# Two blocks of V of one group per layer moved to partitions 0 to 63, in eight transfers on ACT's queue

## The chip, the cores and the metric

The kernel runs on one core of one Trainium2 chip. A core has engines that run their own instruction streams and meet at semaphores: TensorE (PE, matrix products into PSUM), VectorE (DVE), ScalarE (ACT), GpSimd (POOL) and SyncE (SP, here the issuer of transfers). Sixteen DMA engines bring data from HBM into SBUF, a memory of 128 partitions. SP and ACT can each issue transfers, each on a queue of its own that all sixteen engines serve. The metric is the device time of one execution in microseconds; less is better.

## What is computed

One token passes twice through an attention layer over a cache of 4096 keys and an MLP. Everything is float32; the caches K and V (32 heads, 4096 keys, 128 numbers each, 67 MB each) are read twice, once in each layer.

```python
def _A_ref(x, k_cache, v_cache, wq, wo):
    ...
    q = (x @ wq).reshape(B, Sq, H, Dh).transpose(0, 2, 1, 3)
    scores = jnp.einsum("bhqd,bhkd->bhqk", q, k_cache) * (Dh ** -0.5)
    p = _softmax(scores, axis=-1)
    o = jnp.einsum("bhqk,bhkd->bhqd", p, v_cache)
    return o.transpose(0, 2, 1, 3).reshape(B, Sq, H * Dh) @ wo
def _B_ref(x, w1, b1, w2, b2):
    h = _gelu(jnp.einsum("bsd,df->bsf", x, w1) + b1)
    return jnp.einsum("bsf,fd->bsd", h, w2) + b2
x = A_x
x = x + _A_ref(_layernorm(x), A_k_cache, A_v_cache, A_wq, A_wo)
x = x + _B_ref(_layernorm(x), B_w1, B_b1, B_w2, B_b2)
x = x + _A_ref(_layernorm(x), A_k_cache, A_v_cache, A_wq, A_wo)
x = x + _B_ref(_layernorm(x), B_w1, B_b1, B_w2, B_b2)
```

## The kernel before

The 32 heads are worked in eight groups of four (g; n is a group's turn). Layer 0 goes through g = 0 to 7, layer 1 through 7 to 0, so that what is in SBUF at the end of layer 0 (V of g = 7 whole, parts of K and V of g = 6) needn't be read again. All tiles lie in one SBUF array, `arena`; a transfer's place in it is given by hand as a column (`k_home`, `v_home`, in units of `NC` = 2048 columns, 8 KB; `BLOCK` = 8 NC is a whole K or V tile of a group, 128 partitions x 64 KB).

One group's turn is: `stream("k", ...)` loads K, and `scores` (L211) multiplies its eight chunks with the query, 32 products of 512 columns into the PSUM tile `pS`; `softmax` (L216) finds the maximum on DVE, makes the exponential on ACT (L223), turns the weights around with four transposes on PE (L225) and copies them to `pt` (L227); `stream("v", ...)` loads V, and `values` (L239) makes 32 products of 4 x 512 into `pO`: of each chunk, four blocks b of 128 keys for each of four heads j. `scaled_out` (L244) and `head_out` (L266) take the group's result through its part of wo into `pB`, and `queries` (L201) makes the next group's query. Between these, `idle` (L367) issues products whose result nobody uses; six of them stand behind the scores of layer 0's first group (L418 to L420).

Every transfer goes through `load` (L83), on SP's queue in the order in which the program is written, 128 partitions at a time. In the middle of a layer the order is K, V, then wo and the next wq together (`in_w`, L473), then the next group's K. A transfer is issued when the place that it writes is free: V of a group when the products on the K that lay there are done, w when the queries that used the old one are done, in layer 0 the next K when the V that lay there has landed and been used.

The framework gives each transfer the next of eight semaphores (DMAHW0 to DMAHW7), in turn over the order in which it schedules the program, whatever engine issues it. A transfer on a semaphore that is in use waits, on its issuing engine, until the transfer before it on that semaphore has landed. With SP alone, eight transfers lie between two uses.

Of the kernel before, what the change touches and what calls it, by code (L numbers as in the profile page):

```python
# [17 lines left out]
P = 128  # L18
# [3 lines left out]
G = 8  # L22
J = 4
C = 8
# [3 lines left out]
U = 512  # L28
KEPT = 6

NC = 4 * U
BLOCK = 8 * NC

STAY = 5 * NC
SPARE = 2 * BLOCK + STAY
HELD = SPARE + 2 * NC
# [14 lines left out]
FILL = 3  # L51
LAST = ((0, 4), (4, 6), (6, 7))
LAST_IDLE = {3: 1, 5: 1, 6: 1}
WHOLE, HALVES = ((0, 8),), ((0, 4), (4, 8))
VAR_AT = 1


@with_exitstack
def decode_layers(ctx: ExitStack, tc: tile.TileContext, k, v, w, w1, w2, out):
    nc = tc.nc  # L60
# [20 lines left out]
    arena = const.tile([P, ARENA], F32, name="arena")  # L81

    def load(at, src):  # L83
        t = arena[:, at : at + src.shape[-1]]
        tc.keep_in_program_order(nc.sync.dma_start(t, src))
        return t
# [41 lines left out]
    row, _ = wq_at(0)  # L128
# [3 lines left out]
    ident = ctile("ident", P)  # L132
# [7 lines left out]
    pS, pO, pB = (psum.tile([P, 512], F32, name=n) for n in ("pS", "pO", "pB"))  # L140
# [75 lines left out]
    def softmax(sc, nsc, p):  # L216
        nc.vector.tensor_reduce(mx[:, 0:1], pS, axis=AX.X, op=ALU.max)  # L217
        mt, m, bias = small("mt", 32), small("m"), small("lr", 32)
        nc.vector.transpose(mt, mx)
        nc.vector.tensor_reduce(m, mt[:, :C], axis=AX.X, op=ALU.max)  # L220
        nc.vector.tensor_scalar(mb[:, :C], m.to_broadcast([P, C]), nsc, None, op0=ALU.mult)
        nc.vector.transpose(bias, mb)  # L222
        nc.scalar.activation(p, pS, AF.Exp, bias=bias[:, 0:1], scale=sc, accum_out=mx[:, 0:1])  # L223
        for b in range(4):
            nc.tensor.transpose(pT[:, b].rearrange("p j r -> p (j r)"), p[:, P * b : P * (b + 1)], ident)  # L225
        pt = work.tile([P, J, C, 4], F32, name="pt")
        nc.vector.tensor_copy(pt, pT[:, :, :, :C].rearrange("p b j c -> p j c b"))  # L227
        lt, l, lr, rl = small("mt", 32), small("l"), small("lr", 32), small("rl")
        nc.vector.transpose(lt, mx)  # L229
        nc.vector.tensor_reduce(l, lt[:, :C], axis=AX.X, op=ALU.add)  # L230
        nc.vector.tensor_copy(lt, l.to_broadcast([P, 32]))
        nc.vector.transpose(lr, lt)
        nc.vector.reciprocal(rl, lr[:, 0:1])
        return pt, rl

    def by_head(vt):
        return vt.rearrange("p b (j d) -> p j b d", j=J)

    def values(i, pt, vt, c, of=C):  # L239
        for j in range(J):  # L240
            nc.tensor.matmul(pO[32 * j : 32 * j + 4, :], pt[:, j, c, :], by_head(vt)[:, j],  # L241
                             start=(i == 0), stop=(i == of - 1))
# [127 lines left out]
    for layer in range(2):  # L370
# [17 lines left out]
        r = rstd_of(ss, pN[:, 1:2])  # L388
# [4 lines left out]
        for n, g in enumerate(order):  # L393
# [6 lines left out]
            if layer == 1 and n == 0:  # L400
                tiles = [(c, here["k", g, c]) for c in range(C)]
            elif layer == 1 and n == 1:
                tiles = [(c, here["k", g, c]) for c in range(2)]
                tiles += list(stream("k", g, ((2, 4), (4, 8)), -2 * NC))
                n_kept = STAY + U * KEPT
                load(V1_HOME[6] + n_kept % NC, v[g][:, n_kept:BLOCK])
                for u in range(STAY, n_kept - U, U):
                    nc.scalar.copy(v_next(u), pK[(u - STAY) // U])
                for c in range(STAY // NC, C):
                    here["v", g, c] = chunk(arena[:, V1_HOME[c] : V1_HOME[c] + NC])  # L410
            elif layer == 1 and n == 2:
                tiles = [(c, here["k", g, c]) for c in range(6)]
                tiles += list(stream("k", g, ((6, 8),), 2 * BLOCK - 6 * NC))
            else:
                tiles = stream("k", g, HALVES if first or final else WHOLE, k_home)
            for c, t in tiles:
                scores(z, c, t)
            if first or final:  # L418
                for _ in range(FILL if final or layer == 1 else 2 * FILL):
                    idle(t, pO)  # L420
            p, ot = free_now(layer, n)
            if layer == 1 and first:
                z = queries(n + 1, xc_l, wq_next, pO)
                nc.scalar.copy(v_next(STAY + U * KEPT - U), pB)
            pt, rl = softmax(sc, nsc, p)
            if final:
                nc.scalar.activation(small("m"), rl, AF.Gelu_apprx_tanh)

            if layer == 1 and n == 0:
                for c in range(C):  # L430
                    values(c, pt, here["v", g, c], c)
            elif layer == 1 and n == 1:
                for c in range(C):
                    values(c, pt, here["v", g, c], c)

                for pieces, base in ((((0, 4),), K2_HOME), (((4, 6),), SPARE - 4 * NC)):
                    for _ in stream("k", order[2], pieces, base):
                        pass
            elif final:
                last_v = chunk(arena[:, v_home + BLOCK - NC : v_home + BLOCK])  # L440
                for _ in range(FILL - 1):
                    idle(t, pS)
                for c, t in stream("v", g, LAST, v_home):
                    values(c, pt, t, c, C - 1)
                    if c == C - 2:
                        others = scaled_out(rl, ot)
                    for _ in range(LAST_IDLE.get(c, 0)):
                        idle(t, pS)
                for a in (BLOCK - NC, BLOCK - NC // 2):
                    load(v_home + a, v[g][:, a : a + NC // 2])  # L450
                for c in range(C):
                    here["v", g, c] = chunk(arena[:, v_home + NC * c : v_home + NC * (c + 1)])
            else:
                for c, t in stream("v", g, WHOLE, v_home):
                    for i in range(KEPT - 1):
                        if layer == 0 and n == G - 2 and c == (STAY + U * i) // NC:
                            nc.scalar.copy(pK[i], t[:, STAY // U % J + i - J * (c - STAY // NC), :])
                    values(c, pt, t, c)

            if layer == 1 and n == 0:  # L460
                wo_t = chunk(arena[:, PAIR : PAIR + NC])
# [54 lines left out]
        if layer == 0:  # L516
# [4 lines left out]
            g = G - 2  # L521
# [53 lines left out]
```

## Time and profile before

| what | value |
|---|---|
| median of 3 runs | 678.17 us (677.98 to 678.79) |
| the profiled execution | 677.63 us, its span 675.9 us |
| granted TensorE clock, mean | 0.806 |
| PE busy | 408.1 us (60% of the span) |
| DVE / ACT busy | 115.2 us (17%) / 27.4 us (4%) |
| moved from HBM | 284.92 MB, 422 GB/s over the span |

The span is cut into 40 equal slices in the page's second part; a digit there is a busy share in tenths. A row of a timeline reads: start in us, duration in us, engine and line, operation, and in brackets the idle time before it and what ended it. In the chain of waits, "another core or an unknown queue" stands where PE waited for a landing whose transfer the profile doesn't name. SPq is the time in which SP issues a transfer; the bytes follow later on the DMA engines.

### The profile page before, as it was taken

The page shows a single profiled execution, that of the slowest core. Times are in us where ns is not written, and L with a number is a line of the kernel's source. Part 1 is how long each engine was busy: PE and PEld are TensorE (multiplying, and loading weights), DVE is VectorE, ACT ScalarE, POOL GpSimd, SP SyncE. Part 2 cuts the span into 40 slices and gives each one's busy share as a digit, 9 for nine tenths or more (in the row PEclk, how much of TensorE's full clock was granted, in tenths as well). Part 3 has the DMA queues.
Part 4 walks back from the last instruction along what each step waited for, and adds up shares of the span by engine and source line. Part 5 has one row for each costly group of instructions (what it writes and reads, how often), then busy time and mean ns, then how long its engine had stood idle before and what let it go on. Part 6 is the DMA issues. An engine that isn't in the chain of part 4 may idle for free.

```text
span 675.9 us, 6740 instructions
## 1 busy us (share of the span) xinstructions
PE 408.1 (60%) x3008; PEld 109.8 (16%) x3008; DVE 115.2 (17%) x369; ACT 27.4 (4%) x57; POOL 5.0 (1%) x24
## 2 busy tenths in 40 slices
PE   2745664565534854467597986674466545755596
PEld 1111111111111111111124321111111111111123
DVE  3002110120021201212022322120121111200212
ACT  0010000000000000001011200000000000000010
POOL 1000000000000000000000000000000000000000
PEclk9779776797678865878899998976797767976899
DMA  9999999999999999999999999999999999999995
GB/s 374 435 434 434 435 435 434 413 457 432 428 427 422 444 434 432 434 432 417 433 410 353 427 418 462 407 447 435 426 432 431 432 434 409 461 432 411 426 414 234
DMA packets 11268, 285.34 MB, mean 422 GB/s; under 512 B 1252, under 2 KB 1256, under 8 KB 3688
## 3 DMA queue, kind: packets, MB, share of 16 engines
q1 hardware_dynamic: 11240, 284.92, 98.6%
q8 instruction: 23, 0.38, 0.2%
q14 instruction: 5, 0.04, 0.0%
HBM read 284.92 MB, written 0.00 MB: 422 GB/s over the span
## 4 chain that ended last, share of the span: by engine, by line
PE 40%; DMA 39%; another core or an unknown queue 14%; DVE 4%; ACT 1%; issue 1%; ACTq 0%; SPq 0%; DVEq 0%
DMA arena<-in_v 35%; PE pO L241 19%; PE pS L213 12%; DMA arena<-in_w 4%; PE pB L269 4%; PE pO L207 1%; PE pO L225 1%; ACT arena L223 1%; PE pS L368 1%; DVE arena L245 1%; DVE smalls L217 1%; PE pO L368 0%; PE pO L343 0%; DVE arena L205 0%
## 5 line engine op out<-in xcount | busy, mean ns | idle before, releaser
L213 PE MATMUL pS<-arena,smalls 128*8 128x512 f32 x1024 | 148.3, 732 | 112.5 <-DMA arena<-in_k 111.6
L241 PE MATMUL pO<-arena,pt 128*4 128x512 f32 x1008 | 139.9, 700 | 79.1 <-DMA arena<-in_v 78.6
L269 PE MATMUL pB<-arena,smalls 128*1 128x512 f32 x112 | 52.8, 616 | 21.9 <-DVE smalls L250 15.9
L213 PEld LDWEIGHTS pS<-arena,smalls 128*8 128x8 f32 x1024 | 30.1, 103 | 214.9 <-issue 190.9
L241 PEld LDWEIGHTS pO<-arena,pt 128*4 128x4 f32 x1008 | 28.4, 95 | 178.0 <-issue 175.2
L217 DVE TENSOR_REDUCE smalls<-pS 128x1 f32<-128x512 f32 x16 | 11.1, 692 | 253.1 <-PE pS L213 253.1
L245 DVE STREAM_TRANSPOSE arena<-pO 128x512 f32<-128x512 f32 x16 | 11.5, 717 | 217.1 <-PE pO L241 217.1
L223 ACT ACTIVATE arena<-pS,smalls 128x512 f32<-128x512 f32 x16 | 12.4, 778 | 536.2 <-DVE smalls L222 536.2
L205 DVE SCALAR_TENSOR_TENSOR arena<-arena,smalls 128x512 f32<-128x512 f32 x45 | 33.8, 752 | 1.6
L225 PE MATMUL pO<-ident,arena 128*128 128x128 f32 x64 | 13.2, 341 | 33.8 <-ACT arena L223 33.5
L269 PEld LDWEIGHTS pB<-arena,smalls 128*1 128x1 f32 x112 | 8.6, 85 | 65.9 <-issue 38.2
L207 PE MATMUL pO<-smalls,arena 128*128 128x1 f32 x120 | 16.6, 259 | 3.3 <-DVE arena L205 3.3
L207 PEld LDWEIGHTS pO<-smalls,arena 128*128 128x128 f32 x120 | 15.3, 200 | 15.5 <-DVE arena L205 13.8
L225 PEld LDWEIGHTS pO<-ident,arena 128*128 128x128 f32 x64 | 8.5, 169 | 47.7 <-ACT arena L223 46.5
L368 PE MATMUL pO<-arena,ident 128*8 128x512 f32 (+1 forms) x38 | 15.9, 547 | 0.0
L368 PE MATMUL pS<-arena,ident 128*8 128x512 f32 (+1 forms) x34 | 14.0, 517 | 0.5 <-DVE pt L307 0.5
L203 DVE TENSOR_SCALAR arena<-arena,smalls 128x512 f32<-128x512 f32 x15 | 7.2, 480 | 4.7 <-DMA arena<-in_w 4.7
L343 PE MATMUL pO<-arena,smalls 128*1 128x128 f32 x176 | 5.9, 272 | 3.3 <-DMA arena<-in_w 2.2
L208 DVE COPY smalls<-pO 128x4 f32<-128x4 f32 x15 | 2.5, 165 | 26.5 <-PE pO L207 26.5
L169 PE MATMUL pO<-smalls 128*32 128x1 f32 x64 | 2.0, 184 | 7.4 <-DVE smalls L163 6.3
L229 DVE STREAM_TRANSPOSE smalls<-smalls 128x32 f32<-128x32 f32 x16 | 3.4, 211 | 17.5 <-ACT arena L223 17.5
L295 PE MATMUL pS<-arena,smalls 128*2 128x128 f32 (+1 forms) x160 | 4.9, 259 | 1.9 <-DMA arena<-in_w 1.9
(92 smaller groups left out, 101.2 us busy)
## 6 DMA issues: line engine op xcount, KB each, us to landing
arena<-in_k SPq DMA_DIRECT2D x8, 4096.0 KB, 26.0
arena<-in_w SPq DMA_DIRECT2D x13, 2048.0 KB, 33.2
arena<-in_v SPq DMA_DIRECT2D x2, 4096.0 KB, 38.4
arena<-in_k SPq DMA_DIRECT2D x3, 2048.0 KB, 15.9
arena<-in_v SPq DMA_DIRECT2D x2, 2048.0 KB, 41.6
arena<-in_w SPq DMA_DIRECT2D x4, 1024.0 KB, 16.3
arena<-in_w SPq DMA_DIRECT2D x6, 512.0 KB, 13.3
arena<-in_v SPq DMA_DIRECT2D x2, 1024.0 KB, 43.2
```

What stands on the lines that cost most here:

```text
L203: pin(nc.vector.tensor_scalar(t, wt[:, 0, :], xc[:, 0:1], None, op0=ALU.mult))
L205: nc.vector.scalar_tensor_tensor(t, wt[:, c, :], xc[:, c : c + 1], t, op0=ALU.mult, op1=ALU.add)
L207: nc.tensor.matmul(at[:, j : j + 1], t[:, P * j : P * (j + 1)], one, start=True, stop=True)
L213: nc.tensor.matmul(pS[32 * j : 32 * j + C, :], z[:, j, C - 1 - c : 2 * C - 1 - c], kt[:, j, :], start=(c == 0), stop=(c == C - 1))
L217: nc.vector.tensor_reduce(mx[:, 0:1], pS, axis=AX.X, op=ALU.max)
L223: nc.scalar.activation(p, pS, AF.Exp, bias=bias[:, 0:1], scale=sc, accum_out=mx[:, 0:1])
L225: nc.tensor.transpose(pT[:, b].rearrange("p j r -> p (j r)"), p[:, P * b : P * (b + 1)], ident)
L241: nc.tensor.matmul(pO[32 * j : 32 * j + 4, :], pt[:, j, c, :], by_head(vt)[:, j], start=(i == 0), stop=(i == of - 1))
L245: nc.vector.transpose(ot[:, :512], pO)
L269: nc.tensor.matmul(pB[0:1, :], on[:, d : d + 1], wt[:, d, :], start=n == 0 and d == 0, stop=n == G - 2 and d == 3)
L343: pin(nc.tensor.matmul(pM[32 * j : 32 * j + 1, :], g[:, c - b0 : c - b0 + 1], w2_t[c][:, P * j : P * (j + 1)], start=(c == 0), stop=(c == ...
L368: pin(nc.tensor.matmul(at[:C, :n], ident[:, :C], t[:, 0, :n], start=True, stop=True))
```

## The change

In the group g = 3 of each layer (turn n = 3 in layer 0, n = 4 in layer 1; `MOVED_OF`), the last two blocks of 128 keys of V's last chunk are split. V's own transfer is 1024 columns shorter (60 KB of 64 KB a partition). A new function, `load_moved`, brings the two blocks in eight transfers on ACT's queue; transfer q takes the partitions first, first + 4, ... first + 28, eight rows of 2048 columns: 1024 that belong to the partition, and 1024 that belonged to the partition 64 above it, which the host has copied behind the row into its padding. So nothing of these two blocks lies on partitions 64 to 127. `second_half` brings the upper half of the weights of these keys to partitions 0 to 63, with two more transposes on PE into `pO` and a copy on DVE. `values_in_halves` takes the place of `values` for the last chunk: three products of 256 columns for each of four j (lower half, upper half, and the two blocks that stay) in place of one of 512. Six idle products behind the first scores of layer 0 go. In the changed file the lines stand some 4 to 44 further down (`load` at L89).

```diff
+LOWER, MOVED = P // 2, 2
+MOVED_OF = {0: 3, 1: G - 1 - 3}
+MOVED_AT = 3 * BLOCK, SPARE
+HALF_AT = HELD + 2 * NC + U + 4 * 129, SPARE + 2 * MOVED * U
...
+    def load_moved(layer, g):
+        t = arena[:LOWER, MOVED_AT[layer] : MOVED_AT[layer] + 2 * MOVED * U]
+        for q in range(8):
+            first = q % 4 + 32 * (q // 4)
+            rows = slice(first, first + 29, 4)
+            nc.scalar.dma_start(t[rows], v[g][rows, BLOCK - MOVED * U : BLOCK + MOVED * U])
+        return t.rearrange("p (h b j d) -> h p j b d", h=2, b=MOVED, j=J)
+    def second_half(layer, p):
+        for i in range(MOVED):
+            b = 4 - MOVED + i
+            nc.tensor.transpose(pO[:LOWER, P * i : P * (i + 1)], p[:, P * b + LOWER : P * (b + 1)], ident)
+        t = arena[:LOWER, HALF_AT[layer] : HALF_AT[layer] + J * MOVED].rearrange("p (j b) -> p j b", j=J)
+        nc.vector.tensor_copy(t, pO[:LOWER, : P * MOVED].rearrange("p (b j r) -> p j b r", b=MOVED, j=J)[:, :, :, C - 1])
+        return t
+    def values_in_halves(pt, pt_half, vt, moved):
+        b = 4 - MOVED
+        for j in range(J):
+            at = pO[32 * j : 32 * j + 4]
+            nc.tensor.matmul(at[:MOVED, : P * MOVED], pt_half[:, j], moved[1][:, j], start=False, stop=False)
+            nc.tensor.matmul(at[:, P * b :], pt[:LOWER, j, C - 1, :], moved[0][:, j], start=False, stop=False)
+            nc.tensor.matmul(at[:, : P * b], pt[:, j, C - 1, :], by_head(vt)[:, j, :b], start=False, stop=True)
...
+            halved = n == MOVED_OF[layer]
+            if halved:
+                moved = load_moved(layer, g)
             for c, t in tiles:
                 scores(z, c, t)
             if first or final:
-                for _ in range(FILL if final or layer == 1 else 2 * FILL):
+                for _ in range(FILL if final or layer == 1 else 0):
                     idle(t, pO)
...
             pt, rl = softmax(sc, nsc, p)
+            if halved:
+                pt_half = second_half(layer, p)
...
-                for c, t in stream("v", g, WHOLE, v_home):
+                if halved:
+                    t = load(v_home, v[g][:, : BLOCK - MOVED * U])
...
+                    if halved and c == C - 1:
+                        values_in_halves(pt, pt_half, t, moved)
+                    else:
+                        values(c, pt, t, c)
...
+    arrays["v"][3, :LOWER, BLOCK : BLOCK + MOVED * U] = arrays["v"][3, LOWER:, BLOCK - MOVED * U : BLOCK]
```

How the built program's instructions stand, at three places. First SP's transfers in layer 0, before: w and K of n = 3, V of n = 3, w and K of n = 4, V of n = 4. In brackets are the semaphores that a transfer waits for.

```order
L85 DMA arena<-in_w 128x4096 [waits DMAHW7_49,DVE_49,PE_49]
L85 DMA arena<-in_k 128x16384 [waits DMAHW6_49]
L85 DMA arena<-in_v 128x16384 [waits DMAHW0_49,PE_49]
L85 DMA arena<-in_w 128x4096 [waits DMAHW2_49,DVE_49,PE_49]
L85 DMA arena<-in_k 128x16384 [waits DMAHW1_49]
L85 DMA arena<-in_v 128x16384 [waits DMAHW3_49,PE_49]
```

And now:

```order
L89 DMA arena<-in_w 128x4096 [waits DMAHW7_49,DVE_49,PE_49]
L89 DMA arena<-in_k 128x16384 [waits DMAHW6_49]
L89 DMA arena<-in_v 128x15360 [waits DMAHW3_49,DMAHW0_49,PE_49]
L89 DMA arena<-in_w 128x4096 [waits DMAHW2_49,DMAHW5_49,DVE_49,PE_49]
L89 DMA arena<-in_k 128x16384 [waits DMAHW6_49,DMAHW1_49]
L89 DMA arena<-in_v 128x16384 [waits DMAHW7_49,PE_49]
```

No transfer has moved on SP; V of n = 3 waits for DMAHW3 as well, and the three behind it for one more each (DMAHW5, 6) or another (DMAHW7). In layer 1 the same place is V of n = 4, with K of n = 4 ahead of it and w and K of n = 5 behind it; before:

```order
L85 DMA arena<-in_k 128x16384 [waits DMAHW5_49,DMAHW0_49,PE_49]
L85 DMA arena<-in_v 128x16384 [waits DMAHW6_49,PE_49]
L85 DMA arena<-in_w 128x4096 [waits DMAHW2_49,DMAHW7_49,DVE_49,PE_49]
L85 DMA arena<-in_k 128x16384 [waits DMAHW0_49,PE_49]
L85 DMA arena<-in_v 128x16384 [waits DMAHW1_49,PE_49]
```

And now:

```order
L89 DMA arena<-in_k 128x16384 [waits DMAHW5_49,DMAHW0_49,PE_49]
L89 DMA arena<-in_v 128x15360 [waits DMAHW6_49,DMAHW0_49,PE_49]
L89 DMA arena<-in_w 128x4096 [waits DMAHW2_49,DMAHW7_49,DVE_49,PE_49]
L89 DMA arena<-in_k 128x16384 [waits DMAHW3_49,PE_49]
L89 DMA arena<-in_v 128x16384 [waits DMAHW4_49,DMAHW0_49,PE_49]
```

Here V of n = 4 waits for DMAHW0 too. Third, ACT in layer 0 now, from the exponentials of n = 1 and 2 over the eight new transfers to the exponential of n = 3 and after; before, the exponentials followed each other:

```order
L227 ACTIVATE arena,smalls<-pS,smalls 128x512 [waits DVE_49,PE_49,Activation_49] x2
L254 DMA arena<-in_v 8x2048 [waits DMAHW4_49,DMAHW0_49,DVE_49]
L254 DMA arena<-in_v 8x2048 [waits DMAHW5_49]
L254 DMA arena<-in_v 8x2048 [waits DMAHW6_49]
L254 DMA arena<-in_v 8x2048 [waits DMAHW7_49]
L254 DMA arena<-in_v 8x2048 [waits DMAHW0_49]
L254 DMA arena<-in_v 8x2048 [waits DMAHW1_49]
L254 DMA arena<-in_v 8x2048 [waits DMAHW2_49]
L254 DMA arena<-in_v 8x2048 [waits DMAHW4_49]
L227 ACTIVATE arena,smalls<-pS,smalls 128x512 [waits DVE_49,PE_49,Activation_49] x4
```

The eight stand between two exponentials and take the semaphores in turn from DMAHW4 to DMAHW2 and DMAHW4 again; DMAHW3, left out among them, is the one on which V of n = 3 goes.

More of the change, by code (lines that the diff above doesn't have):

```diff
@@ L453, in decode_layers @@
             else:
-                for c, t in stream("v", g, WHOLE, v_home):
+                if halved:
+                    t = load(v_home, v[g][:, : BLOCK - MOVED * U])
+                    pieces = [(c, arena[:, v_home + NC * c : v_home + NC * (c + 1)]) for c in range(C)]
+                    pieces = [(c, t.rearrange("p (b n) -> p b n", n=U)) for c, t in pieces]
+                for c, t in pieces if halved else stream("v", g, WHOLE, v_home):
                     for i in range(KEPT - 1):
@@ L457, in decode_layers @@
                             nc.scalar.copy(pK[i], t[:, STAY // U % J + i - J * (c - STAY // NC), :])
-                    values(c, pt, t, c)
+                    if halved and c == C - 1:
+                        values_in_halves(pt, pt_half, t, moved)
+                    else:
+                        values(c, pt, t, c)
             if layer == 1 and n == 0:
```

## Prediction

> **What bounds the kernel now.** I read the page first (span, slices, queues, chain), then SP's timeline at the two changed groups, then the count of packets in short windows, which tells how far the sixteen DMA engines are apart.
>
> ```profile
> span 675.9 us, 6740 instructions
> DMA  9999999999999999999999999999999999999995
> GB/s 374 435 434 434 435 435 434 413 457 432 428 427 422 444 434 432 434 432 417 433 410 353 427 418 462 407 447 435 426 432 431 432 434 409 461 432 411 426 414 234
> q1 hardware_dynamic: 11240, 284.92, 98.6%
> q8 instruction: 23, 0.38, 0.2%
> ```
>
> The DMA engines are busy in every slice, and one queue (SP's) holds 98.6% of their time: the kernel is bound by its 285 MB. At 434 GB/s an engine moves 27.1 GB/s. Three things can change the time: bytes per engine, time in which the queue is empty, and how unevenly the engines finish, since a transfer has landed only when its slowest engine is done. PE's waits are for landings, so the end of layer 0 and of the program are landings too:
>
> ```profile
> 353.52 11.31 DMA arena<-in_w
> 364.87 0.83 PE pS L295 x32
> ...
> 658.91 13.33 DMA arena<-in_w
> 672.28 0.66 PE pO L343 x16
> ```
>
> The queue never empties because SP issues far ahead. In layer 0 (group n=3) and layer 1 (n=4), from SP's timeline and from PE's rows:
>
> ```profile
> 123.83 0.33 SPq L85 DMA_DIRECT2D arena<-in_v  x1
> 147.91 0.33 SPq L85 DMA_DIRECT2D arena<-in_w  x1
> 148.29 0.42 SPq L85 DMA_DIRECT2D arena<-in_k  x1
> 157.39 4.81 PE L213 MATMUL pS<-arena,smalls 128*8 128x512 f32 x28 [9.50 <-DMA arena<-in_k]
> 176.88 5.30 PE L241 MATMUL pO<-arena,pt 128*4 128x512 f32 x28 [7.40 <-DMA arena<-in_v]
> ...
> 496.21 0.33 SPq L85 DMA_DIRECT2D arena<-in_v  x1
> 502.07 0.33 SPq L85 DMA_DIRECT2D arena<-in_w  x1
> 520.29 0.33 SPq L85 DMA_DIRECT2D arena<-in_k  x1
> 510.73 9.49 PE L213 MATMUL pS<-arena,smalls 128*8 128x512 f32 x64 [8.69 <-DMA arena<-in_k]
> ```
>
> V of n=3 is issued at 123.8, 33 us before K of n=3 has landed (PE starts on it at 157.4) and so 33 us before the queue would run dry. In layer 1, V of n=4 is issued at 496.2, 14 us before K of n=4 lands (510.7).
>
> **The change: a wait that empties the queue.** The order rows show what decides. The eight new transfers on ACT take a whole turn of the eight completion semaphores, and V's own transfer falls on the semaphore of the K just ahead of it: DMAHW3 in layer 0, DMAHW0 in layer 1. That these belong to that K is seen in the rows of before, where V of n=4 waits for DMAHW3 and layer 1's next K for DMAHW0, each because it overwrites that K. So V of n=3 can't be issued at 123.8 any more but only when K of n=3 has landed; its w and the next K stand behind it on SP. Nothing else of SP's is then in flight: the queue is empty once in each layer. The price of starting an empty queue is in the first transfer of the program (a window of the first 6 us in 40 slices of 0.15 us, with SP's issue and the median to landing):
>
> ```profile
> 0.72 0.39 SPq L85 DMA_DIRECT2D arena<-in_w  x1
> GB/s 0 0 0 0 0 0 0 0 0 0 0 338 169 113 0 169 56 56 507 394 394 394 451 394 451 338 563 338 507 394 394 394 394 1966 1529 0 0 0 0 0
> arena<-in_w SPq DMA_DIRECT2D x1, 1056.0 KB, 4.9
> ```
>
> Full rate begins at slice 18, 2.70 us; the slices ahead of it moved 901 x 0.15 = 135 KB, worth 0.31 us. So 2.70 - 0.31 - 0.72 = 1.7 us are lost from issue on. The other bound is the landing: 4.9 us less 1.08 MB at 434 GB/s (2.5 us) = 2.4. I take **2.0 us** for each stop.
>
> **Bytes.** Each of the eight new transfers brings 8 rows of 8 KB, one row an engine if it runs on eight engines: 64 KB, 2.42 us, on each of eight engines. V's rows are 4 KB shorter: 8 x 4 KB = 32 KB, **1.21 us** less on all sixteen. That only as many engines as rows take part, I read from the last transfer (4 rows; window 673.5 to 675.5), against a K tile of 128 rows, which ends with sixteen packets under 512 B (window 24.3 to 24.9):
>
> ```profile
> DMA packets 8, 0.00 MB, mean 1 GB/s; under 512 B 4, under 2 KB 8, under 8 KB 8
> ...
> DMA packets 32, 1.05 MB, mean 1748 GB/s; under 512 B 16, under 2 KB 16, under 8 KB 16
> ```
>
> [...]
>
> ACT reaches the new transfers behind its exponential of the group before. The semaphores that they wait for belong to transfers that stand ahead of this K in SP's queue, so their bytes pass beside K, before the stop.
>
> **How far the engines are apart.** Sixteen packets under 512 B end a transfer, one an engine. In this order: V of n=0 (43.7 to 44.0 and 45.2 to 45.5, its last), K of n=3 (155.1 to 155.5 and 156.5 to 157.0), K's second half at the end of layer 0 (329.8 to 330.2 and 332.7 to 333.1), layer 1's K of n=4 (506.6 to 507.6 and 509.9 to 510.3), the program's end (666.6 to 667.2 and 671.4 to 672.0):
>
> ```profile
> DMA packets 20, 0.16 MB, mean 546 GB/s; under 512 B 10, under 2 KB 10, under 8 KB 10
> DMA packets 4, 0.05 MB, mean 164 GB/s; under 512 B 1, under 2 KB 1, under 8 KB 1
> ...
> DMA packets 24, 0.79 MB, mean 1966 GB/s; under 512 B 12, under 2 KB 12, under 8 KB 12
> DMA packets 6, 0.20 MB, mean 393 GB/s; under 512 B 3, under 2 KB 3, under 8 KB 3
> ...
> DMA packets 14, 0.29 MB, mean 737 GB/s; under 512 B 5, under 2 KB 5, under 8 KB 5
> DMA packets 5, 0.13 MB, mean 328 GB/s; under 512 B 1, under 2 KB 1, under 8 KB 1
> ...
> DMA packets 18, 0.59 MB, mean 590 GB/s; under 512 B 9, under 2 KB 9, under 8 KB 9
> DMA packets 3, 0.13 MB, mean 328 GB/s; under 512 B 1, under 2 KB 1, under 8 KB 1
> ...
> DMA packets 45, 0.22 MB, mean 372 GB/s; under 512 B 4, under 2 KB 4, under 8 KB 43
> DMA packets 3, 0.01 MB, mean 14 GB/s; under 512 B 1, under 2 KB 1, under 8 KB 3
> ```
>
> After one fetch of instructions (q8) one engine is about 1.5 us behind the rest; at K of n=3 it is still 1.5 at most, with twelve engines together; 2.9 at the end of layer 0; in layer 1 about 3.2 at K of n=4 and 4.8 at the end. So between the stop's place and the layer's end the slowest engine falls back by one fetch, 1.5 us, in both layers. A stop lines the engines up again, and by the layer's end one fetch puts some engine 1.5 us behind: the growth behind the stop is the same with and without it and drops out. What is left for a layer is
>
> d + 2.0 - 1.21,
>
> with d how much later K's slowest engine lands because of the 2.42 us. If the late engines of layer 0 are not among the eight: the twelve lie within 0.4, so 0.3 + 2.42 - 1.5 = 1.2; if they are, 2.42. The middle is 1.8. In layer 1 between 0 (the eight are among the nine within 1.0 of the first: 0.8 + 2.42 is no more than 3.2) and 2.42; I take 1.2. The sum is (1.8 + 0.8) + (1.2 + 0.8) = **4.6 us**.
>
> **Packets of a second queue.** No row shows two load queues at once. Below: a packet between others costs its bytes alone, 0. Above: the fetch, also another queue's packet, cost its engine 1.5 us less the earlier spread of 0.2, against 16 KB / 27.1 = 0.6: 0.7 more. I take 0.1 a packet, nearest to the lower end, because a fetch doesn't end in the arena and a load does, and SP's own transfers follow each other at 434 GB/s. 16 packets an engine: **1.6 us** (0 to 11). [...]
>
> **What is hidden.** PE: two more transposes (0.33, half of four in 0.66), one DVE copy (0.29), and the last chunk's 12 products of 256 columns for 4 of 512, half as much again of 1.1 us (8.85 / 32 x 4): 0.55. The first two lie in PE's wait of 7.40 us above; the 0.55 comes behind V's landing, when w and K of the next group (2.1 and 8.4 MB, 24 us at 434 GB/s) are queued. Uncovered, both layers would cost 2.4 us. ACT's eight issues (0.33 to 0.42 us each on SP, about 3 in all) and waits lie in a wait of 41 us. The idle products:
>
> ```profile
> 133.13 8.85 PE L241 MATMUL pO<-arena,pt 128*4 128x512 f32 x64 [5.50 <-DMA arena<-in_v]
> 168.82 0.66 PE L225 MATMUL pO<-ident,arena 128*128 128x128 f32 x4 [2.76 <-ACT arena L223]
> 127.66 0.29 DVE L227 COPY pt<-pO 128x128 f32<-128x128 f32 x1 [0.29 <-PE pO L225]
> 167.90 0.78 ACT L223 ACTIVATE arena<-pS,smalls 128x512 f32<-128x512 f32 x1 [41.43 <-DVE smalls L222]
> 31.44 5.31 PE L368 MATMUL pO<-arena,ident 128*8 128x512 f32 x12
> 45.88 1.89 PE L241 MATMUL pO<-arena,pt 128*4 128x512 f32 x8 [8.54 <-DMA arena<-in_v]
> ```
>
> The six take 5.3 us ahead of a wait of 8.5 us for V. Without them the wait grows; should PE's clock fall for the next products, the DMA row has no empty slice there, so nothing of it reaches the end. Nothing either way.
>
> **The sum** is made against this execution: 677.63 us with a span of 675.9 (1.7 around it); 677.63 + 6.2 = 683.8. It lies 0.54 below the median 678.17, so I forecast **684.4 us**, from 680 to 688 for this case (0.70).
>
> **Rivals.** (a) **Faster, 675.8 (0.09).** The eight engines that get less are the late ones, and V's wait costs nothing. Each layer then gains the 1.21 us that the late engines lose, 2.4 in all. It decides at one point: whether K's semaphore is met when SP reaches V, at 123.8; PE's row has K's landing at 157.4, which speaks against it. For it: the last three engines at 157 are over a microsecond behind twelve, so moving 1.2 us from them is the right size. (b) **Slower by far, 689 to 694 (0.12).** ACT's packets cost as much as a fetch's: 16 x 0.35 to 0.7 = 5.6 to 11.2 on top of 4.6. For it: the fetch row; against: above. (c) **No change, 677 to 679.5 (0.09).** Stops as short as 1.7 with d = 0 in layer 1 and 1.2 in layer 0 still leave 1.7 + 0.5 = 2.2; to stay below 1.4 a stop must cost under 1.3 or the lined-up engines must be spared a fetch until the end.
>
> **How the numbers follow.** A measurement here can tell about 0.2%, 1.4 us: slower is above 679.5, faster below 676.8. Slower holds the forecast and (b), 0.82, and a little of (c) beyond the bound: 0.84; same 0.07; faster 0.09. The range 679.6 to 690.5 leaves out (a), most of (c) and the end of (b).
>
> **What would show it.** In the new trace SP's issue of V right behind K's landing (near 159 and 512) instead of 33 and 14 us ahead; a gap of about 2 us in the DMA row there; V of n=3 landing some 3 to 4 us later than 176.7; layer 1 starting 2 to 3 us later; the engines together after each stop. A second queue with 128 packets of 8 KB and their time tells its price. The prediction is wrong if V is issued before K's landing, or if the bytes on eight engines are not the ones that K's landing waits for.

## The result and the profile after

The changed kernel takes **683.31 us** (median of 6 runs, 681.9 to 684.02); the kernel before, on the same chip, 678.08 (677.0 to 678.79). The ratio is 1.0075, 95% interval 1.0062 to 1.0089: **5.2 us slower**, where 684.4 was forecast with 679.6 to 690.5. The profiled execution of after took 681.9 us, the lowest of its six; its span is 3.9 us longer than that of before, so the trace shows some three quarters of the loss. The sizes in this section are those of the trace.

The page of after, with the lines that answer to those of before:

```profile
span 679.8 us, 6830 instructions
DMA  9999999998999999999999999999999999999996
GB/s 374 434 433 443 441 432 441 425 431 356 424 444 425 447 440 432 433 437 405 429 409 350 428 422 445 422 443 432 432 425 370 422 436 415 446 429 428 431 411 268
q1 hardware_dynamic: 11240, 283.88, 97.8%
q10 hardware_dynamic: 256, 1.05, 0.4%
q8 instruction: 23, 0.38, 0.2%
```

Two dips are new, 356 GB/s in the tenth slice and 370 in the thirty-first; q10 is ACT's queue. SP's issues, ACT's issues and PE's starts on K and V at the two places (start, duration, engine and line):

```profile
157.52 0.33 SPq L89 DMA_DIRECT2D arena<-in_v  x1
158.01 0.33 SPq L89 DMA_DIRECT2D arena<-in_w  x1
158.43 0.47 SPq L89 DMA_DIRECT2D arena<-in_k  x1
...
512.67 0.33 SPq L89 DMA_DIRECT2D arena<-in_v  x1
513.16 0.33 SPq L89 DMA_DIRECT2D arena<-in_w  x1
...
144.19 10.33 ACTq L254 DMA_DIRECT2D arena<-in_v  x8
...
157.58 9.71 PE L217 MATMUL pS<-arena,smalls 128*8 128x512 f32 x64 [8.53 <-DMA arena<-in_k]
179.89 6.65 PE L245 MATMUL pO<-arena,pt 128*4 128x512 f32 x44 [7.70 <-DMA arena<-in_v]
...
512.75 9.62 PE L217 MATMUL pS<-arena,smalls 128*8 128x512 f32 x64 [10.68 <-DMA arena<-in_k]
534.11 8.32 PE L245 MATMUL pO<-arena,pt 128*4 128x512 f32 x56 [6.85 <-DMA arena<-in_v]
```

V is issued at 157.5 in place of 123.8 and at 512.7 in place of 496.2, each within 0.1 us of PE's start on the K ahead of it. In layer 0 w and the next K follow at once, as they had been ready; in layer 1 w does. In the chain of waits (start, duration, what it is) V of n=4 stood in before with its whole wait in the queue; in after, K's landing, V's issue and V's landing follow each other without a gap. First before, then after:

```profile
496.21 33.75 DMA arena<-in_v
```

```profile
478.02 34.60 DMA arena<-in_k
512.67 21.30 DMA arena<-in_v
```

How much moved at the two places, in windows of 154 to 161 and 508 to 517 us (the last two numbers of a row: busy share of the DMA engines, GB/s), first before, then after:

```profile
154.00:161.00 7.00, 3.61 (x20) 0.75 (x24) 0.00 (x0) 0.00 (x0) 0.00 (x0) 0.52 1.02 440
508.00:517.00 9.00, 6.27 (x36) 1.29 (x40) 0.00 (x0) 0.00 (x0) 0.00 (x0) 0.57 1.03 444
```

```profile
154.00:161.00 7.00, 3.42 (x20) 0.70 (x24) 0.00 (x0) 0.00 (x0) 0.00 (x0) 0.50 0.67 242
508.00:517.00 9.00, 4.25 (x23) 0.84 (x27) 0.00 (x0) 0.00 (x0) 0.00 (x0) 0.50 0.79 302
```

In the first window 198 GB/s are missing over 7 us, 1.4 MB or 3.2 us at 434 GB/s; in the second 142 over 9 us, 1.3 MB or 2.9 us. Together that is 6.1 us, more than the 3.9 by which the span grew; what gives the rest back is taken up in the part on the prediction.

The trace also has each engine's completion of each transfer. This table, made from them for before, after and four kernels of the next section, gives the landing of a transfer on its last engine and, in brackets, how far the first was ahead, in us:

| kernel | K n=3, layer 0 | V n=3 | last of layer 0 (w1) | K n=4, layer 1 | V n=4 | last load (w2) |
|---|---|---|---|---|---|---|
| before | 157.25 (1.63) | 176.74 (1.77) | 364.82 (3.16) | 510.60 (3.40) | 529.96 (3.40) | 672.24 (4.93) |
| after | 157.44 (1.81) | 179.75 (2.15) | 366.43 (2.20) | 512.62 (2.41) | 533.98 (1.18) | 675.88 (2.36) |
| stop_only | 157.26 (1.81) | 179.55 (1.03) | 367.76 (2.59) | 513.59 (2.62) | 536.00 (1.07) | 678.25 (2.57) |
| stop_covered | 157.50 (2.10) | 181.75 (1.96) | 365.00 (3.41) | 511.83 (2.44) | 536.08 (2.36) | 673.48 (3.84) |
| no_stop | 158.59 (3.00) | 177.19 (3.44) | 364.81 (4.41) | 513.89 (4.49) | 532.47 (4.91) | 674.73 (6.44) |
| half_moved | 158.25 (2.58) | 177.14 (2.71) | 365.32 (4.22) | 511.21 (2.41) | 529.98 (2.43) | 672.24 (3.94) |

From before to after V of n=3 lands 3.0 us later, of which 1.4 are gone by the end of layer 0: before's engines come 1.4 further apart on the way (1.77 to 3.16), after's do not (2.15 to 2.20). V of n=4 is 4.0 later, the last load 3.6.

### The profile page after: what moved, and what is told of

It reads as the page before. It is cut to its first block, busy times and chain, and to the rows that moved or that the text cites. A ratio compares the mean times of both kernels' runs of the same rounds, so it can differ in the third digit from the quotient of the medians.

```text
span 679.8 us, 6830 instructions
## 1 busy us (share of the span) xinstructions
PE 415.0 (61%) x3032; PEld 111.7 (16%) x3032; DVE 115.5 (17%) x371; ACT 27.4 (4%) x57; POOL 5.0 (1%) x24
## 3 DMA queue, kind: packets, MB, share of 16 engines
q10 hardware_dynamic: 256, 1.05, 0.4%
## 4 chain that ended last, share of the span: by engine, by line
DMA 58%; PE 25%; another core or an unknown queue 13%; DVE 2%; issue 1%; ACT 0%; SPq 0%; ACTq 0%; DVEq 0%
DMA arena<-in_v 32%; DMA arena<-in_k 18%; PE pO L245 10%; DMA arena<-in_w 8%; PE pS L217 7%; PE pB L300 3%; PE pO L211 1%; PE pO L374 1%; PE pO L273 1%; PE pO L271 1%; PE pS L399 1%; PE pO L272 1%; DVE arena L276 0%; PE pO L399 0%
## 5 line engine op out<-in xcount | busy, mean ns | idle before, releaser
L217 PE MATMUL pS<-arena,smalls 128*8 128x512 f32 x1024 | 145.8, 721 | 101.0 <-DMA arena<-in_k 100.2
L245 PE MATMUL pO<-arena,pt 128*4 128x512 f32 x992 | 144.1, 723 | 87.2 <-DMA arena<-in_v 86.8
L300 PE MATMUL pB<-arena,smalls 128*1 128x512 f32 x112 | 50.3, 592 | 18.5 <-DVE smalls L281 15.8
L399 PE MATMUL pO<-arena,ident 128*8 128x512 f32 (+1 forms) x26 | 10.6, 527 | 0.0
L374 PE MATMUL pO<-arena,smalls 128*1 128x128 f32 x176 | 7.3, 297 | 2.3 <-DMA arena<-in_w 1.7
```

The lines of the kernel that those rows point to most:

```text
L217: nc.tensor.matmul(pS[32 * j : 32 * j + C, :], z[:, j, C - 1 - c : 2 * C - 1 - c], kt[:, j, :], start=(c == 0), stop=(c == C - 1))
L300: nc.tensor.matmul(pB[0:1, :], on[:, d : d + 1], wt[:, d, :], start=n == 0 and d == 0, stop=n == G - 2 and d == 3)
L374: pin(nc.tensor.matmul(pM[32 * j : 32 * j + 1, :], g[:, c - b0 : c - b0 + 1], w2_t[c][:, P * j : P * (j + 1)], start=(c == 0), stop=(c == ...
L399: pin(nc.tensor.matmul(at[:C, :n], ident[:, :C], t[:, 0, :n], start=True, stop=True))
```

## The experiments

Twelve kernels ran. The median of before in their comparisons was 677.8 to 678.3 us.

### Is it the stop? Undone, and done alone

**no_stop** undoes the stop and keeps all else. Four of the eight transfers are written one turn earlier, so that V falls on the semaphore of another transfer.

```diff
-    def load_moved(layer, g):
+    def load_moved(layer, g, parts):
...
-        for q in range(8):
+        for q in parts:
...
+            if n + 1 == MOVED_OF[layer]:
+                load_moved(layer, order[n + 1], range(4))
             if halved:
-                moved = load_moved(layer, g)
+                moved = load_moved(layer, g, range(4, 8))
```

> The changed kernel with four of the eight ACT transfers written one turn earlier, so that V no longer falls on the semaphore of the K just ahead and SP issues it early again; the same bytes, the same engines, the same products. Theory (the emptied queue costs 2.0 us in each layer, and the engines that lose 4 KB a row are the late ones): the two stops go, SP issues V about 30 us ahead of K's landing, and the time is 675.5 to 677, 6 to 8 us below the changed kernel's 683.3 and 1 to 2.5 below the kernel before. Rival A (eight engines that must bring 64 KB more, a second queue, or the finer products cost the time): 681.5 to 684. Rival B (the stop counts, but the extra bytes cost their 1.21 us in each layer besides): 679.5 to 681.

679.08 us (678.14 to 681.15, 11 runs), ratio to before 1.0022 (1.0011 to 1.0033). SP issues V early again, and the windows hold no gap:

```profile
122.92 0.33 SPq L89 DMA_DIRECT2D arena<-in_v  x1
...
498.21 0.33 SPq L89 DMA_DIRECT2D arena<-in_v  x1
...
154.00:161.00 7.00, 2.27 (x12) 0.48 (x16) 0.00 (x0) 0.00 (x0) 0.00 (x0) 0.50 1.04 446
508.00:517.00 9.00, 2.97 (x16) 0.65 (x20) 0.00 (x0) 0.00 (x0) 0.00 (x0) 0.50 1.04 448
```

Undoing the stops gives back 683.3 - 679.1 = 4.2 us, 2.1 a stop. The result lies between the theory and rival A and nearest to rival B: about 1.2 us remain over before (679.08 less 677.9), and the gain that the theory saw in relieving the late engines is not there.

**stop_only** makes the stop in the kernel before, with 28 KB that nothing reads.

```diff
+    def load_nothing(layer, g):
+        t = arena[: P // 2, (3 * BLOCK, SPARE)[layer] : (3 * BLOCK, SPARE)[layer] + 128]
+        for q in range(7):
+            first = q % 4 + 32 * (q // 4)
+            rows = slice(first, first + 29, 4)
+            nc.scalar.dma_start(t[rows], v[g][rows, BLOCK : BLOCK + 128])
...
+            if n == (3, 4)[layer]:
+                load_nothing(layer, g)
```

> The kernel before with seven small transfers on ACT (eight rows of 512 bytes of padding, 28 KB in all, into columns that nothing reads) at the two places, so that V falls on the semaphore of the K just ahead; V's bytes, its products and the idle products stay as before. Theory (the emptied queue, 2.0 us in each layer): SP issues V behind K's landing, near 159 and 512 us, and the time is 681 to 683, 3 to 5 us above the kernel before. Rival (the time comes from the moved bytes and the finer products): 677.5 to 679, as before.

684.38 us (683.77 to 685.29, 4 runs), ratio 1.0093 (1.008 to 1.0106): 6.5 us above before, more than was expected and more than the change itself costs.

```profile
157.34 0.33 SPq L85 DMA_DIRECT2D arena<-in_v  x1
...
154.00:161.00 7.00, 3.60 (x20) 0.82 (x24) 0.00 (x0) 0.00 (x0) 0.00 (x0) 0.50 0.54 184
508.00:517.00 9.00, 3.27 (x16) 0.65 (x20) 0.00 (x0) 0.00 (x0) 0.00 (x0) 0.50 0.66 250
```

By the table V of n=3 lands 2.8 us later than before, V of n=4 another 3.1 later (6.04 less the 2.99 that K of n=4 is late already). The first engine has V at 178.52 (179.55 less 1.03), 21.18 us after its issue at 157.34; eight rows of 64 KB are 8 x 2.42 = 19.36, so the start takes 1.8 us. The last engine follows 1.03 behind. The packets show both. Behind the issue at 157.34 the sixteen engines' first packets of V begin between 158.31 and 159.27, and they take 2.67 to 3.84 us in place of 2.42; in layer 1, behind the issue at 513.66, they begin between 514.62 and 515.98.

**stop_covered** keeps the wait and fills the queue. It has six small transfers in place of seven, and w of the next group is written ahead of V, so that V still waits for the K on its semaphore while w's 2.1 MB are moved.

```diff
-        for q in range(7):
+        for q in range(6):
...
+                if n == (3, 4)[layer]:
+                    t_w = load(PAIR, of_w(wo_at(g) if layer == 0 else wq_at(g - 1), 2))
                 for c, t in stream("v", g, WHOLE, v_home):
...
-                t = load(PAIR, of_w(wo_at(g) if layer == 0 else wq_at(g - 1), 2))
+                t = t_w if n == (3, 4)[layer] else load(PAIR, of_w(wo_at(g) if layer == 0 else wq_at(g - 1), 2))
```

> The kernel before with six small transfers on ACT (512 bytes a row) at the two places, and w of the next group written ahead of V there. V still waits for the K just ahead on the same semaphore and is issued behind its landing, but w's 2.1 MB, 4.9 us, are in the queue meanwhile. Theory (only an emptied queue costs; 2.0 us to start plus about 1 us by which the engines come apart at the start): 677.5 to 679, as before. Rival (the wait itself, or the small packets on a second queue, cost 3 us in each layer): 682 to 685.

678.88 us (677.49 to 679.4, 11 runs), ratio 1.0003 (0.9995 to 1.0012): as before.

```profile
148.80 0.33 SPq L85 DMA_DIRECT2D arena<-in_w  x1
157.56 0.33 SPq L85 DMA_DIRECT2D arena<-in_v  x1
...
154.00:161.00 7.00, 3.37 (x17) 0.65 (x20) 0.00 (x0) 0.00 (x0) 0.00 (x0) 0.50 1.02 429
508.00:517.00 9.00, 5.04 (x24) 0.98 (x28) 0.00 (x0) 0.00 (x0) 0.00 (x0) 0.50 0.98 417
```

V is issued at 157.56, as late as with the stop, and it costs nothing that these runs can tell. So it is the empty queue that costs, not the late issue, the wait or the small packets. The medians of the two kernels are 5.5 us apart, 2.75 for each stop; measured against the runs of before beside each (ratios 1.0093 and 1.0003) it is 6.1 us, 3.05 for each, and the landings gave 2.8 and 3.1.

### The idle products, and the moved bytes without the stop

**idles_kept** is the changed kernel with the six idle products put back (`2 * FILL` in place of 0).

> The changed kernel with the six idle products of layer 0 put back. Theory (they lie in a wait for a landing and cost nothing either way): 682.6 to 684, the changed kernel's time. Rival (without them PE's clock falls and that costs a part of the loss): 680 to 682.

683.3 us (681.28 to 684.29, 6 runs), ratio to before 1.0071 (1.0057 to 1.0084): the changed kernel's time. They cost and bring nothing.

The trace of no_stop then raised a doubt: at 363 us the same 32 products took 1.89 us where they took 1.05 before, and layer 1 started 1.3 us later. **no_stop_idles** puts the six products back there.

> The kernel without the stop (four of the eight ACT transfers a turn earlier) with the six idle products of layer 0 put back. In its trace without them, 32 products at the end of layer 0 took 1.89 us at 363.2 where they took 1.05 before, and PE reached layer 1's first K 1.3 us later. Theory (the missing idle products shift the granted clock, which costs some 1.3 us at the change of layer where PE sets the pace, and the moved bytes themselves come out at nothing): 677.3 to 678.4, as before. Rival (that stretch falls as it will, and the moved bytes cost 1 us): 678.6 to 679.6.

679.64 us (678.24 to 680.82, 12 runs), ratio 1.002 (1.001 to 1.0029). The theory falls: the same products took 1.88 us with the idle products too, and the time is that of no_stop. These products at the end of layer 0 in before, no_stop_idles and half_moved (the next kernel), all three with the six idle products:

```profile
363.23 1.05 PE L343 MATMUL pO<-arena,smalls 128*1 128x128 f32 x32 [1.44 <-DMA arena<-in_w]
```

```profile
363.26 1.88 PE L374 MATMUL pO<-arena,smalls 128*1 128x128 f32 x32 [1.00 <-DMA arena<-in_w]
```

```profile
363.75 1.05 PE L374 MATMUL pO<-arena,smalls 128*1 128x128 f32 x32 [1.44 <-DMA arena<-in_w]
```

The granted clock from 355 to 365 us was 1.00, 0.74 and 0.83. So the six products do not set it. The change of layer has a loss of its own, though. At the last w that lands ahead of layer 1's moved bytes (447.61 in before) no_stop is 1.18 us late and no_stop_idles 1.20, though both were level with before at the end of layer 0. stop_covered, which moves no bytes and also took 1.89 us there, loses 1.04 over the same stretch, half_moved 0.10. The 32 products alone don't tell it: they took 1.89 us in after too, which loses nothing there (1.61 late at the end of layer 0, 1.20 at that w). By the last load no_stop is 2.49 late and no_stop_idles 2.27. About half of what these two traces lose thus arises where no moved byte is in flight.

**half_moved** is no_stop_idles with one block of keys moved in place of two (`MOVED` = 1): the same split products in number, half of the bytes.

> The kernel without the stop, the idle products put back, with one block of 128 keys moved in place of two: eight engines bring 32 KB more and all sixteen 16 KB less. Theory (with two blocks the eight engines that carry them become the late ones, by as much as the others are relieved; half of it stands between the two): 676.6 to 677.8, 0.3 to 1 below the kernel before. Rival (moving bytes between the halves changes nothing of the time): 677.6 to 678.6.

678.2 us (677.33 to 680.06, 12 runs), ratio 1.0002 (0.9992 to 1.0011). That is 1.4 us below no_stop_idles, with as many finer products, so these are not what was left. Whether it is all due to the second block's bytes is not shown: in the traces the last loads of the two are 2.27 us apart, and 1.08 of these arise at the change of layer. The hoped gain was not found. The table shows the engines' part in it: with two blocks in no_stop the first and the last engine are 3.00 apart at K of n=3 (before 1.63) and 6.44 at the end (4.93), with one block 2.58 and 3.94. The packets of no_stop tell which engines are late at K of n=3. Eight of K's sixteen completing packets begin 5 to 6 ns after one of ACT's, as packets of one engine follow each other; they come at 156.87 to 157.94 us, the other eight at 155.15 to 156.89. With two blocks the engines that carry the bytes have become the late ones.

### One transfer, and which rows

**one_transfer** brings the moved bytes in one transfer of 64 rows.

```diff
-        for q in range(8):
-            first = q % 4 + 32 * (q // 4)
-            rows = slice(first, first + 29, 4)
-            nc.scalar.dma_start(t[rows], v[g][rows, BLOCK - MOVED * U : BLOCK + MOVED * U])
+        nc.scalar.dma_start(t, v[g][:LOWER, BLOCK - MOVED * U : BLOCK + MOVED * U])
```

> The changed kernel with one ACT transfer of 64 rows in place of the eight of eight rows; the split products, the transposes and the removal of six idle products stay. Then V waits for nothing new, and the moved bytes lie on all sixteen engines alike. Theory (the stop is the cost): 677.3 to 678.7, as before. Rival (the split products or the missing idle products cost the time): 681.5 to 684.

684.05 us (683.38 to 684.46, 4 runs), ratio 1.0086 (1.0073 to 1.0099), just above the rival's range, but not for its reason. ACT issues the transfer much earlier (9.4 and 431.3 us), SP issues V at 125.6 without a stop, and the loss stands beside the transfer: in 434 to 449 us the DMA engines are busy and move a third less than behind it (windows of 434 to 449 and 460 to 480 us).

```profile
434.00:449.00 15.00, 0.66 (x4) 0.42 (x4) 2.40 (x11) 0.87 (x2) 0.00 (x0) 0.62 0.96 291
460.00:480.00 20.00, 10.21 (x52) 2.81 (x56) 3.62 (x8) 0.00 (x0) 0.00 (x0) 0.74 1.01 437
```

SP's packets, 27.1 GB/s an engine elsewhere, ran at 14 to 24 there. In 9 to 20 us, beside the first of the two transfers, 343 GB/s moved where before moved 429. So the run doesn't tell what it was made for, and raised a question of its own: why don't the eight transfers of the change do this? Four kernels change no_stop in which rows a transfer has, and a fifth tries the spacing of four on the other half of the partitions. **no_stop_rows** takes eight neighbours:

```diff
-            first = q % 4 + 32 * (q // 4)
-            rows = slice(first, first + 29, 4)
+            first = 8 * q
+            rows = slice(first, first + 8)
```

> The kernel without the stop, the six idle products left out, with eight neighbouring rows in each ACT transfer (8q to 8q + 7) in place of every fourth. With one transfer of 64 rows an engine's rate beside it had fallen from 27.1 to between 14 and 20 GB/s for some 15 us. If it is the engines' number that does it (all sixteen at once there, eight here): the rate stays at 27 and the time at 678.5 to 680. If it is which rows an engine writes (neighbouring rows by engines that otherwise write elsewhere): the rate falls again and the time is 682 to 686.

690.71 us (689.54 to 691.73, 4 runs), ratio 1.0183 (1.0168 to 1.0197), above the second theory's range: the rows decide, not the number of engines. The first eight of these transfers were also issued from 9.3 us on, where no_stop issues its first at 99.8, so **rows_later** keeps them behind ACT's exponentials.

> Neighbouring rows again (8q to 8q + 7), but kept behind ACT's exponentials, so that the transfers run beside K and V of 64 KB a row, as the spaced ones do, and not at the program's start. Theory (neighbouring rows slow every engine, wherever they fall): SP's packets beside each transfer of 8 rows at about 17 to 21 GB/s an engine, 0.6 to 0.8 us lost for each of 16, 687 to 692. Rival (the early place made the loss): 27 GB/s throughout and 678.5 to 680.

689.78 us (689.15 to 692.06, 4 runs), ratio 1.0179 (1.0157 to 1.02): the place is not the cause. **rows_by_2** and **rows_by_8** are no_stop with every second row (over 16 partitions) and every eighth row (over 64) in a transfer.

> The kernel without the stop, with every second row in a transfer (spread over 16 partitions) in place of every fourth (32 partitions). Theory (what counts is how many partitions lie between the rows that the engines write together): a loss between that of neighbouring rows and none, 680.5 to 686. Rival (only neighbouring rows clash): 678.5 to 680.

> [...] Theory (rows four apart are far enough already): 678.5 to 680, as with every fourth. Rival (four apart still costs something, in which case the 1.2 us by which the kernel without the stop stays behind the kernel before is of this kind): 677 to 678.3.

687.15 us (686.03 to 688.07, 4 runs), ratio 1.0133 (1.0114 to 1.0152), and 688.27 (687.49 to 689.46, 4 runs), ratio 1.0154 (1.0134 to 1.0173). The theory of distance falls with the second: eight apart is as bad as two, and of the spacings tried only four is free. The same stretch (100 to 125 us) of no_stop, rows_by_2 and rows_by_8, with the first four transfers in it:

```profile
100.00:125.00 25.00, 13.61 (x80) 3.42 (x80) 4.31 (x10) 0.26 (x1) 0.00 (x0) 0.80 0.99 428
```

```profile
100.00:125.00 25.00, 13.27 (x80) 3.31 (x78) 2.31 (x5) 0.00 (x0) 0.00 (x0) 0.73 0.97 391
```

```profile
100.00:125.00 25.00, 13.41 (x80) 3.32 (x78) 2.54 (x5) 0.00 (x0) 0.00 (x0) 0.73 0.99 391
```

The engines are busy all the time and move 428, 391 and 391 GB/s. V is issued early in all of these kernels (124.7 to 130.3 and 503.4 to 508.8 us), so no stop is in their loss. **upper_rows** then tried the other half: the kernel before, with sixteen transfers that nothing reads, every fourth row, but of partitions 64 to 127.

```diff
+        t = arena[:, at : at + 4 * U]
+        for q in parts:
+            first = P // 2 + q % 4 + 32 * (q // 4)
+            rows = slice(first, first + 29, 4)
+            nc.scalar.dma_start(t[rows], v[g][rows, BLOCK - 2 * U : BLOCK + 2 * U])
```

> The kernel before with sixteen transfers of eight rows on ACT that nothing reads, every fourth row and at the places of the kernel without the stop, but on partitions 64 to 127; V, its products and the idle products stay as before, and no stop is made. Four layouts of eight rows have been seen: every fourth row of partitions 0 to 63 leaves SP's packets at 27.1 GB/s, rows 1, 2 or 8 apart slow them. [...]

689.27 us (688.73 to 691.12, 4 runs), ratio 1.0177 (1.016 to 1.0193), and 397 GB/s in the same stretch. The author forecast 682.5 to 688 if SP's packets were slowed here too, and 679 to 682 if they kept 27 GB/s an engine. V keeps its whole rows here, so the extra bytes, 64 KB on each of eight engines in each layer, would have cost up to 4.8 us by themselves (an estimate: twice 64 KB at the 27.1 GB/s of one engine in before); the loss is 11.4 (689.27 less 677.89, the kernel before beside it), and some 6.5 us lie beyond that.

```profile
100.00:125.00 25.00, 13.52 (x80) 3.40 (x78) 2.43 (x5) 0.00 (x0) 0.00 (x0) 0.73 0.98 397
```

SP's packets of 64 KB took up to 2.9 us there, with a quarter of them over 2.77, where three quarters took no more than 2.43 in no_stop. Spacing alone is not enough, then: of the layouts of eight rows that were tried only every fourth row of partitions 0 to 63 leaves SP's packets as they are (679.1 us; the others took 687.2 to 690.7). What makes it so is not shown: no packet of a trace names its engine, and every layout reads the same rows of HBM that it writes in SBUF, so the reading side was not tried by itself. upper_rows reads at the spacing of the free layout and is slow, which speaks against the spacing of the reads alone.

## Why the prediction came out right, and what in it was wrong

**The wait that empties the queue: shown.** V is issued behind K's landing, at 157.5 and 512.7, its w behind it; made alone the wait costs 6.5 us, filled with other work nothing, and undone it gives back 4.2. The forecast signs came in part: the late issue, the gap, and V of n=3 landing 3.0 us later. Layer 1 began only 1.2 to 1.6 us later where 2 to 3 were forecast, and the engines were not together behind the stop (2.15 us apart at V of n=3, before 1.77).

**Its price: mis-sized, 2.0 forecast, 2.75 to 3.1 measured.** The start itself took 1.8 us, near the 1.7 that the prediction read from the program's first transfer. What it had wrong is "A stop lines the engines up again". They don't come off together: V's completions lie 1.03 us apart in layer 0 and 1.07 in layer 1 after a stop (stop_only), so a stop is 1.8 to start and about 1 for the engines that start late. One of the late ones in layer 0 follows a fetch of instructions (158.26, 0.93 us); why the others start late was not tried. The rest of that step, that the growth behind the stop is the same with and without it, held in stop_only (1.77 to 3.16 in before, 1.03 to 2.59 here, both about 1.5 by the end of layer 0). It did not hold in after, whose spread in layer 0 did not grow.

**d, the bytes beside K: wrong.** The prediction had them "pass beside K, before the stop", 1.8 and 1.2 us; K's landing is 0.19 and 0.83 later (512.62 less 510.60, less the 1.19 by which V of n=3 in layer 1, two transfers ahead of it, was late already). Two things were missed. The first new transfer waits on DVE as well, which the order rows showed: ACT issues it at 144.19, as DVE ends the group before, not at 126 behind the exponential. And each small packet waits its turn behind a packet of 64 KB: one engine's row of packets in after is 8 KB at 148.22, 64 KB at 148.53, ACT's completing packet at 150.96, 64 KB at 150.96, 8 KB at 153.38. Of after's 128 packets of the first eight transfers (64 of 8 KB, 64 that complete), only 18 had passed by 155, eleven us after the first issue, and 111 ran between 154 and 161 (windows of 146 to 155 and 154 to 161, which share one):

```profile
DMA packets 70, 3.49 MB, mean 388 GB/s; under 512 B 8, under 2 KB 8, under 8 KB 8
q10 hardware_dynamic: 18, 0.08, 2.2%
...
DMA packets 147, 1.70 MB, mean 242 GB/s; under 512 B 72, under 2 KB 72, under 8 KB 72
q10 hardware_dynamic: 111, 0.45, 15.8%
```

Most of the bytes moved at K's end and in the stop, on engines that had nothing else; the last of them ended at 158.68, as V's first packets began. So V's 32 KB less an engine stayed as a gain: from K's landing to the layer's last landing after takes 208.99 and 163.26 us, stop_only 210.50 and 164.66. That is 1.5 and 1.4 less, and makes the change cheaper than its stop alone: 5.2 against 6.5.

**The second queue's packets: 1.6 forecast, nothing found.** The 8 KB packets took 309 to 320 ns in no_stop, 8 KB at 26 GB/s, and SP's 64 KB packets beside them no more than 2.43 us (104 to 119 us). The lower end of the bound, a packet between others costs its bytes alone, was the right one, and rival (b) falls; but only for these rows. With other rows a transfer of 64 KB cost the program 0.5 to 0.7 us (rows_by_2 less no_stop, 8.1 us, over 16 transfers; neighbouring rows 11.6 over 16).

**The bytes: right in after, less so without the stop.** The 1.21 us less of V are borne out, as just said. That a transfer of eight rows loads eight engines and not all is borne out by its eight completing packets (64 for eight transfers) and by the spread of 3.00 at K of n=3 in no_stop. Without the stop 1.2 to 1.3 us were left in both layers together, where the terms gave 0.6 (d of 1.8 and 1.2, less 1.21 each); a part of them may be the change of layer.

**Rival (a), 675.8 without the stop:** that V's wait costs nothing was made true in no_stop, and the time was 679.1. The eight engines with 64 KB more each became the late ones, and with half of the bytes the time is that of before.

**What was hidden:** the idle products (683.30 and 683.31 us with and without) and the split products (half_moved, with half of the bytes, takes the time of before) cost nothing that was found, as said.

**The sum.** Forecast 6.2 = stops 4.0 + d 3.0 - bytes 2.4 + packets 1.6. Found: stops 5.5 to 6.1, d 0.2 + 0.8 = 1.0, bytes -2.4 to -2.9, packets nothing, together 3.6 to 4.7; measured were 5.2 between the medians and 3.6 between the last loads of the two traces. The cause was right, and so was the term of the bytes. The stops were 1.5 to 2.1 too small, d and the packets 3.6 too large, and these errors offset each other: that the number came so near is in part luck.

## What to carry to other kernels

Where a framework hands out completion semaphores in turn, count the transfers between two uses: a burst of small ones on another engine can make the next large one wait for the transfer just ahead of it, as eight did here (V issued at 157.5 in place of 123.8 us). Such a wait cost nothing here while 2.1 MB of something else were queued (678.88 us, ratio 1.0003), and 2.1 to 3.1 us when nothing was; writing another ready transfer ahead of it was enough. Before taking bytes from one set of DMA engines, see how far these are behind the others. Here the engines lay 1.63 us apart at K of n=3; the eight that got the moved bytes (64 KB, 2.42 us at 27.1 GB/s) became the late ones, and the spread 3.00 us (no_stop).

## What was not expected of the hardware

- A second queue's small transfers can slow the first queue's packets while the engines stay busy (0.96 to 0.99 of the time): 428 GB/s with every fourth row of partitions 0 to 63, 391 with every second or eighth row, 397 with every fourth row of the other half, 291 beside one transfer of 64 rows. From 104 to 119 us two thirds or more of SP's 64 KB packets took over 2.45 us with every second or eighth row or on the other half, and none in no_stop.
- A packet of 8 KB on one queue waits behind one of 64 KB on the other: in after one of 8 KB at 148.22 was followed by 64 KB at 148.53 and 64 KB at 150.96 before the next at 153.38; in no_stop a transfer of 64 KB issued at 101.1 landed at 108.4, the three behind it at 113.5, 116.3 and 121.4.
- A restarted queue doesn't start its engines together: in stop_only their first packets began 0.96 and 1.37 us apart, and 1.03 and 1.07 us lay between the first and the last engine at the end of the next 8 MB.
- PE's same 32 products at the change of layer took 1.05 us in some kernels and 1.88 to 1.89 in others; with the six idle products in place both occurred. no_stop, no_stop_idles and stop_covered, three of those with the longer time, lost about 1 us at the change of layer, and after lost nothing there. What decides stays open.
